# A fused retention and rational-MLP kernel: signs by a rectifier's slope, small constants in one transfer, 11 unread products, and a new early order

## The chip, the core and the metric

One core of a Trainium2 chip runs the whole program. The metric is device time in microseconds (us) of one execution, compared by the median of several. TensorE is called PE, VectorE DVE, ScalarE ACT, GpSimd POOL and SyncE SP, as in the profile. SP issues all data transfers. Each engine works through its own list of instructions in the order in which the program wrote them, and stops at an instruction whose inputs are not ready.

## What is computed

The reference first runs a retention layer: 8 batches, 8 heads, 576 tokens, 64 channels, with a decay per head in place of a softmax. Its output feeds a two-layer network with a rational function between the layers.

```
scores = (1/8) * q @ k^T;  ret = scores * Dmat[h]      # Dmat = gamma[h]^(i-j) for i >= j, else 0
x = (ret @ v) as [4608 tokens, 512]
h = x @ w_in                                           # w_in [512, 2048]
P = a0 + a1 h + a2 h^2 + a3 h^3
Q = 1 + |b0| |h| + |b1| h^2
out = (P / (Q + 1e-6)) @ w_out                         # w_out [2048, 512]
```

The two weight matrices arrive as 64-bit floats and are turned into 32-bit ones on the chip. All else is 32-bit.

## The kernel before

**Tiling.** The 4608 tokens are 36 units of 128 tokens (`NU`), and 9 blocks of 512 tokens (`NB`). A unit's q and k come as one transfer of 512 KB (`qk`), its k and v in the other layout as another (`kv`). Each of the 16 column groups of a weight matrix (`NF`) is a transfer of 512 KB (`bits`). An operand of the two large products is split in a high and a low part, so a step (one block, one column group) makes 12 products of 128x512 for `h` and 12 for the output `acc`. There are 144 steps.

**The early stage.** The first 8 units (`EARLY`) go through `attention`. For each: `scale_q` (POOL, q times a table `gq`), `scores` (PE), `decay` (DVE, mask), `scale_v` (DVE, v times a table `gv`), `outputs` (PE: `ps<-s,kv` and `ps<-kv`), `cross` (PE, with the state `S_sb`), `keep_hi` (ACT, `xhi`) and `keep_lo` (DVE, `xlo`), `grow` (DVE, adds to `S_sb`) and `fade` (POOL, scales `S_sb`). Cross of unit n waits for the fade of the unit before, so the units form a chain. Two PSUM buffers (`acc`) hold two units at a time. The first 4 units make block 0. Between these units stand the first steps.

**Weights.** `weight` turns one `bits` tile into a high and a low part. `begin` (ACT) takes the absolute value of the high words and scales it, `digit` (ACT) takes bits out of the low words into a tile `t`, `join` (DVE) shifts and ors the two, `sign` (DVE) ors the sign bit back, `high_part` (ACT, sometimes DVE) and `low_part` (POOL or DVE) make `w`.

**A step.** `feed_forward` writes the two products and between them, on ACT and DVE: `p_begin` (a3 h + a2), `size` (|h|), `p_mul`, `p_mul2`, `v_line` (b1 u + b0), `v_mul`, `log`, `exp`, `quot`, `check`, `better`, `g_hi`, `g_lo`. The first 24 steps are `early` (`IN_BANK`). `v_mul` of the first four is on POOL (`V_POOL`). The other 28 units are handled by `late_visit` between steps.

**What sets the order.** Nothing waits for an explicit schedule at run time. While the program is built, `Plan.run` plays the queues: every task has a due time (`DUE`, `FIRST`, `UNITS`), a cost and predecessors, and at each turn the engine that could start soonest writes its next instruction. `LOADS` sets the order of the early transfers. So `DUE`, `FIRST`, `LOADS`, the costs in `add` and the lags (`LAG`, `BACK`) together set the order on each engine.

**The start.** `WARM` products of zeros by zeros into a PSUM tile `unread` run before any data is there. Every instruction is recorded at line 71, the line of a helper, so tiles and not lines tell instructions apart.

Of the kernel before, what the change touches and what calls it, by code (L numbers as in the profile page):

```python
# [34 lines left out]
V_POOL = range(4)  # L35
IN_BANK = 24
WARM = 8
AHEAD = -6
REACH = 7.4
FIRST = (-30.37, -29.34, -25.59, -24.33, -24.08, -16.98, -16.13, -17.66)  # L40
UNITS = (20.48, 2.58, -2.5)
LATE = {'scale': -1.0, 'decay': 0.201, 'middle': 0.3, 'grow': 0.524, 'fade': 0.6, 'keep_hi': 0.3, 'keep_lo': 0.5}
LEAD = -2.2
CNV = 3
CNT = 1
SHIFT = 60
LOADS = 'w0 0 gq mask 1 w1 gv 2 w2 3 w4 w5 w3 5 4 ab w7 6 w9 w6 w10 w8 7 w11'.split()
# [53 lines left out]
class Plan:  # L101
# [19 lines left out]
    def run(self):  # L121
# [14 lines left out]
        dma, left, now, reach = 0.0, len(self.tasks), -2.0, REACH  # L136
        while left:
            best = None
            for e, queue in wait.items():
                found = []  # L140
                for t in queue:
                    if e != "SP" and t.due > now + reach:
                        continue
                    names = [r for r, _ in t.takes]
                    ready = [self.rings[r].ready(names[:j].count(r)) for j, r in enumerate(names)]
                    if None in ready:
                        continue
                    _, _, shared, hold = t.ways[e]
# [45 lines left out]
def retention_ffn(ctx: ExitStack, tc: tile.TileContext, qk, kv, w_in, w_out, ab, masks, masks2, gq, gv, out):  # L194
# [8 lines left out]
    cnt = ctx.enter_context(tc.tile_pool(name="cnt", bufs=CNT))  # L203
# [13 lines left out]
        "qk": 2, "kv": 2, "xp": 2, "cnv": CNV, "t": CNT, "v": 2, "u": 2, "p": 3, "g": 3, "o0": 1, "o1": 1,  # L217
# [12 lines left out]
    qc = const.tile([P, 1], F32, name="qc")  # L230
# [27 lines left out]
    bits, parts, joins = {}, {}, []  # L258
# [3 lines left out]
    def weight(order, s, w, f, loaded):  # L262
# [7 lines left out]
        def begin():  # L270
            c_[0] = cnv.tile([P, DM], I32, tag="c", name=f"c{nm}")
            act.activation(c_[0].bitcast(F32), words()[1].bitcast(F32), AF.Abs, scale=math.ldexp(1.0, -112))

        def digit():
            c_[1] = cnt.tile([P, DM], I32, tag="t", name=f"t{nm}")
            act.activation(c_[1], words()[2], AF.Copy, scale=15 * 2.0**-17)

        def join():
            dve.scalar_tensor_tensor(c_[0], c_[0], 3, c_[1], ALU.logical_shift_left, ALU.bitwise_or)

        def sign():
            dve.scalar_tensor_tensor(c_[0], words()[1], -0x80000000, c_[0], ALU.bitwise_and, ALU.bitwise_or)
# [16 lines left out]
        def low_part_v():  # L299
# [3 lines left out]
        t = add("ACT", d + DUE["begin"], 0.55, begin, [loaded], [("cnv", k)])  # L303
        t = add("ACT", d + DUE["digit"], 0.55, digit, [t], [("t", k)])
        t = add("DVE", d + DUE["join"], 0.61, join, [t], [], [("t", k)], True)
        joins.append(t)
        t = add("DVE", d + DUE["sign"], 0.61, sign, [t], shared=True)
        hi = add("ACT", d + DUE["high_part"], 0.53, high_part, [t], other=[("DVE", 0.5, high_part_v, True)])
        w_ready[k] = hi, add(
            "POOL", d + DUE["low_part"], 1.21, low_part, [hi], [], [("cnv", k)], True, [("DVE", 0.61, low_part_v, True)]  # L310
# [20 lines left out]
    def load_unit(n, due, after=()):  # L331
# [4 lines left out]
        def of(w, nm):  # L336
# [12 lines left out]
            add("SP", due + 0.01 * w, 524 / 390.0, of(w, nm), after, [] if late else [(nm, n)])  # L349
# [9 lines left out]
    def scale(n, at_, got, consts):  # L359
        def scale_q():  # L360
            q, _ = qk_of(n)
            pool.tensor_tensor(q, q, gq_sb, ALU.mult)

        def scale_v(by=dve):
            _, v = kv_of(n)
            dec = gv_sb[:, (n >= EARLY) * H : (n >= EARLY) * H + H].unsqueeze(2).broadcast_to([P, H, D])
            by.tensor_tensor(v, v, dec, ALU.mult)

        def scale_v_p():
            scale_v(pool)  # L370

        tq = add("POOL", at_(DUE["scale_q"]), 1.21, scale_q, [got[0], consts["gq"]], shared=True)
        tv = add("DVE", at_(DUE["scale_v"]), 0.6, scale_v, [got[1], consts["gv"]], shared=True,
                 other=[("POOL", 1.21, scale_v_p, True)])
        return tq, tv

    def attention(n, d, gap, got, consts, prev):
# [121 lines left out]
        th = add("ACT", at_(DUE["keep_hi"]), 0.5, keep_hi, done, [("xp", b)] if n % 4 == 0 else [], gives,  # L499
# [27 lines left out]
    def visit(n):  # L527
        m, heads = n + 1, [(j, g) for j in range(2) for g in range(NPAIR)]
        if "ps" not in late_s:
# [5 lines left out]
        if m < NU:  # L535
            bank["s"] = ps_h.tile([P, 512], F32, tag="h", name=f"ps{n}")
# [15 lines left out]
        if n >= EARLY:  # L552
# [17 lines left out]
    def decay(n):  # L570
        scr[n] = cnv.tile([P, 2, NPAIR, D], F32, tag="c", name=f"s{n}")
# [52 lines left out]
    def late_visit(n, d, got, consts, prev, hold):  # L624

        old, m = n >= EARLY, n + 1
        new, u = m < NU, (n + 1) % 9
        tq = tv = None
        if new:
            dn = d + LATE["scale"]  # L630
            tq = add("POOL", dn, 1.21, lambda: pool.tensor_tensor(qk_of(m)[0], qk_of(m)[0], gq_sb, ALU.mult),
# [7 lines left out]
            def scale_v_p():  # L639
# [3 lines left out]
                     other=[("POOL", 1.21, scale_v_p, True)])  # L643
        key = f"ps{n}"
        tm = te = None
        if m in sooner:
            tm = add("DVE", d - 1.5, 0.42, named(middle, m), [prev["visit"], prev.get("fade")])
        if n + 2 in sooner:
# [14 lines left out]
            "PE", d, (1.7 if m in sooner and n % 9 != 8 else 2.2) if old and new else 1.2, named(visit, n),  # L663
# [355 lines left out]
```

## Time and profile before

| | us |
|---|---|
| median of 3 runs | 899.9 (898.13 to 900.02) |
| the profiled execution | 900.45 |
| its span, first to last instruction | 898.6 |
| PE busy in it | 882.8 (98%) |
| DVE, ACT, POOL busy | 790.4, 653.2, 163.7 |

The page gives busy time per engine, then 40 slices of the span, the transfer queues, the chain of work that ended last, and the costliest groups of instructions. Rows of a timeline read: start, length, engine, line, operation, output<-input, count, and in brackets the idle time of the engine just before and what ended it. Two instructions that follow each other on ACT or DVE overlap a little, so the distance of their starts is some 0.1 us below the length of one.

### The profile page before, as it was taken

How to read it: one execution, taken by the hardware profiler on the slowest of the kernel's cores; microseconds unless marked ns; L12 is line 12 of the kernel's file. 1: busy time of each engine (PE TensorE's matmuls, PEld its weight loads, DVE VectorE, ACT ScalarE, POOL GpSimd, SP SyncE). 2: the span in 40 equal slices, each digit the busy share in tenths (PEclk: the TensorE clock that was granted, in tenths of full speed). 3: DMA queues.
4: the chain of work that ended last, by engine and by line, in shares of the span. 5: the costliest groups of instructions: out<-in, count | busy, mean ns of one | idle time of the engine just before them, and what ended most of it. 6: DMA issues, size and time to landing. Idle time of an engine off the chain costs nothing.

```text
span 898.6 us, 17725 instructions
## 1 busy us (share of the span) xinstructions
PE 882.8 (98%) x7344; PEld 730.3 (81%) x7344; DVE 790.4 (88%) x1215; ACT 653.2 (73%) x1019; POOL 163.7 (18%) x141
## 2 busy tenths in 40 slices
PE   6999999999999999999999999999999999999998
PEld 5777888887888888888888888888888888888886
DVE  4899999988999888988989888988888888987976
ACT  3589999965667767666766677767676786767765
POOL 3565664522211100011101110001100001000000
PEclk9999999999999999999999999999999999999999
DMA  9991000033311112111211131112211021001001
GB/s 357 407 406 69 1 1 1 0 112 123 109 49 61 58 34 70 41 47 60 95 48 48 59 107 48 48 47 74 80 48 47 26 74 44 1 1 47 1 1 47
DMA packets 22641, 67.41 MB, mean 75 GB/s; under 512 B 2592, under 2 KB 4512, under 8 KB 22560
## 3 DMA queue, kind: packets, MB, share of 16 engines
q1 hardware_dynamic: 22560, 66.28, 20.6%
q8 instruction: 57, 0.93, 0.4%
q14 instruction: 24, 0.20, 0.1%
HBM read 56.83 MB, written 9.44 MB: 74 GB/s over the span
## 4 chain that ended last, share of the span: by engine, by line
PE 92%; DVE 3%; DMA 3%; issue 0%; SPq 0%; ACT 0%; POOL 0%; ACTq 0%; DVEq 0%; POOLq 0%
PE acc L71 42%; PE h L71 42%; PE ps L71 7%; DMA bits<-in_w_in 2%; DVE p L71 1%; DMA kv<-in_kv 1%; SPq L71 0%; DVE c L71 0%; DVE s L71 0%; DVE kv L71 0%; DVE xlo L71 0%; DVE v L71 0%; ACT xhi L71 0%; ACT o L71 0%; DVE g L71 0%
## 5 line engine op out<-in xcount | busy, mean ns | idle before, releaser
L71 PE MATMUL acc<-w,g 128*128 128x512 f32 x1632 | 394.2, 390 | 0.0
L71 PEld LDWEIGHTS acc<-w,g 128*128 128x128 f32 x1632 | 305.5, 188 | 64.2 <-POOL w L71 0.4
L71 PE MATMUL h<-xhi,w 128*128 128x512 f32 x1152 | 310.6, 392 | 0.8 <-DVE p L71 0.7
L71 PEld LDWEIGHTS h<-xhi,w 128*128 128x128 f32 x1152 | 213.9, 188 | 47.4 <-DVE p L71 2.1
L71 ACT ACTIVATE p<-h,ab_sb 128x512 f32<-128x512 f32 x143 | 110.8, 775 | 90.7 <-PE h L71 88.5
L71 PE MATMUL h<-xlo,w 128*128 128x512 f32 x576 | 154.2, 390 | 0.0
L71 DVE TENSOR_TENSOR p<-p,h 128x512 f32<-128x512 f32 x144 | 98.4, 683 | 53.8 <-ACT u L71 50.9
L71 DVE SCALAR_TENSOR_TENSOR p<-p,ab_sb,h 128x512 f32<-128x512 f32 x168 | 124.5, 744 | 10.6 <-ACT u L71 8.0
L71 PEld LDWEIGHTS h<-xlo,w 128*128 128x128 f32 x576 | 108.1, 188 | 23.0
L71 ACT ACTIVATE g<-p 128x512 fp32r<-128x512 f32 x136 | 85.6, 629 | 46.5 <-DVE p L71 44.3
L71 ACT ACTIVATE u<-v,qc 128x512 f32<-128x512 f32 x120 | 86.7, 723 | 44.4 <-DVE v L71 44.4
L71 ACT ACTIVATE v<-u,absb 128x512 f32<-128x512 f32 x124 | 101.1, 815 | 3.6
L71 DVE SCALAR_TENSOR_TENSOR p<-p,ab_sb,u 128x512 f32<-128x512 f32 x120 | 95.7, 798 | 4.3 <-ACT u L71 4.3
L71 ACT ACTIVATE u<-h 128x512 f32<-128x512 f32 x144 | 84.8, 589 | 10.5 <-DVE v L71 5.7
L71 DVE SCALAR_TENSOR_TENSOR p<-v,p 128x512 f32<-128x512 f32 x120 | 86.4, 720 | 3.9
L71 DVE TENSOR_TENSOR v<-v,u 128x512 f32<-128x512 f32 x120 | 83.1, 693 | 4.3 <-ACT v L71 3.2
L71 DVE SCALAR_TENSOR_TENSOR v<-v,u 128x512 f32<-128x512 f32 x120 | 84.6, 705 | 0.0
L71 DVE TENSOR_TENSOR g<-p,g 128x512 fp32r<-128x512 f32 x112 | 77.3, 690 | 3.8 <-ACT g L71 2.9
L71 ACT ACTIVATE u<-u 128x512 f32<-128x512 f32 x120 | 75.0, 625 | 2.1
L71 POOL TENSOR_TENSOR qk<-qk,gq_sb 128x512 f32<-128x512 f32 x36 | 49.4, 1374 | 84.6 <-DMA qk<-in_qk 75.9
L71 PEld LDWEIGHTS ps<-qk 64*64 64x64 f32 (+1 forms) x1024 | 38.0, 146 | 18.8 <-issue 10.4
L71 POOL TENSOR_TENSOR S_sb<-S_sb,gv_sb 128x256 f32<-128x256 f32 x18 | 15.7, 872 | 191.7 <-DVE S_sb L71 190.0
(58 smaller groups left out, 766.3 us busy)
## 6 DMA issues: line engine op xcount, KB each, us to landing
qk<-in_qk SPq DMA_DIRECT2D x36, 512.0 KB, 3.9
kv<-in_kv SPq DMA_DIRECT2D x36, 512.0 KB, 5.2
bits<-in_w_in SPq DMA_DIRECT2D x16, 512.0 KB, 10.1
bits<-in_w_out SPq DMA_DIRECT2D x16, 512.0 KB, 10.2
out<-o SPq DMA_DIRECT2D x14, 512.0 KB, 3.3
out<-o SPq DMA_DIRECT2D x8, 256.0 KB, 2.3
x<-in_kv SPq DMA_DIRECT2D x7, 256.0 KB, 5.1
gq_sb<-in_gq SPq DMA_DIRECT2D x1, 256.0 KB, 6.5
```

The costliest lines, as they stand in the source:

```text
L71: return lambda *a, **k: self.tc.keep_in_program_order(method(*a, **k))
```

## The change

**Signs.** `begin` no longer takes an absolute value. It runs a parametric rectifier with slope -2^32 in place on the high words: a negative number comes out positive, with an exponent larger by 32, and the left shift by 3 in `join` puts that into the sign bit. `digit` writes in place too. `sign` and the tile `t` are gone: 32 DVE instructions.

**Small constants.** `gq`, `gv`, the second mask and `a`, `b` come as one array `factors` (602 columns, 301 KB) in one transfer, the first of all. There were four transfers.

**Operands of ACT.** In the early steps `p_begin` and in those not on POOL `v_line` multiply only, and the constant is added in `p_mul` and `v_mul`, which become three-operand instructions on DVE. `log` takes its constant as an immediate number, so the tile `qc` is gone.

**POOL.** `v_mul` of steps 0 to 5, 10, 11 and 17 is on POOL, where it was 0 to 3. All 32 low parts of weights are on POOL, where it was 28.

**Unread products.** `WARM` is 11, was 8.

**Order.** `LOADS`, `DUE`, `FIRST` and the lags have new values, and the queue model in `Plan.run` is changed: a limit of 8 outstanding transfers, two pauses of the transfer queue (`FETCH`), and a delay of DVE behind POOL (`PORT`). Of the tables two lines stand here, since their values tell a reader nothing. Code for visits of early units (`DENSE`, `VISITS`) is in the diff too, but with `DENSE = 8` and `VISITS = ()` it writes nothing.

```
-LOADS = 'w0 0 gq mask 1 w1 gv 2 w2 3 w4 w5 w3 5 4 ab w7 6 w9 w6 w10 w8 7 w11'.split()
+LOADS = 'gq 0 mask 1 0v 2 1v 2v 3 w0 5 3v 5v w2 w1 w5 4 w4 6 w3 w6 4v w9 w7 w11 w10 7v 7 6v w8'.split()
-V_POOL = range(4)
+V_POOL = (0, 1, 2, 3, 4, 5, 10, 11, 17)
-WARM = 8
+WARM = 11
...
-    mask2_sb = const.tile([P, D], F32, name="mask2_sb")
-    gv_sb = const.tile([P, 2 * H + NPAIR], F32, name="gv_sb")
-    gq_sb = const.tile([P, NPAIR, P], F32, name="gq_sb")
-    ab_sb = const.tile([P, 6], F32, name="ab_sb")
+    fac = const.tile([P, 512 + 2 * H + NPAIR + D + 6], F32, name="fac")
+    gq_sb = fac[:, 0:512].rearrange("p (g i) -> p g i", g=NPAIR)
...
         def begin():
+            x = words()[1].bitcast(F32)
+            act.activation(x, x, AF.Prelu, scale=math.ldexp(1.0, -112), alpha=-math.ldexp(1.0, 32))
+
+        def digit():
+            act.activation(words()[0], words()[2], AF.Copy, scale=15 * 2.0**-17)
+
+        def join():
             c_[0] = cnv.tile([P, DM], I32, tag="c", name=f"c{nm}")
-            act.activation(c_[0].bitcast(F32), words()[1].bitcast(F32), AF.Abs, scale=math.ldexp(1.0, -112))
-
-        def digit():
-            c_[1] = cnt.tile([P, DM], I32, tag="t", name=f"t{nm}")
-            act.activation(c_[1], words()[2], AF.Copy, scale=15 * 2.0**-17)
-
-        def join():
-            dve.scalar_tensor_tensor(c_[0], c_[0], 3, c_[1], ALU.logical_shift_left, ALU.bitwise_or)
-
-        def sign():
-            dve.scalar_tensor_tensor(c_[0], words()[1], -0x80000000, c_[0], ALU.bitwise_and, ALU.bitwise_or)
+            dve.scalar_tensor_tensor(c_[0], words()[1], 3, words()[0], ALU.logical_shift_left, ALU.bitwise_or)
...
-            act.activation(e["p"], hs[key], AF.Identity, bias=a2, scale=a3)
+            if early:
+                act.activation(e["p"], hs[key], AF.Copy, scale=a3)
...
-            dve.tensor_tensor(p, p, hs[key], ALU.mult)
+            if early:
+                dve.scalar_tensor_tensor(p, p, a2, hs[key], ALU.add, ALU.mult)
...
-            act.activation(e["line"], e["u"], AF.Identity, bias=b0, scale=b1)
+            if in_bank:
+                act.activation(e["line"], e["u"], AF.Copy, scale=b1)
...
-            (pool if v_pool else dve).tensor_tensor(e["v"], e["line"], e["u"], ALU.mult)
+            if in_bank:
+                dve.scalar_tensor_tensor(e["v"], e["line"], b0, e["u"], ALU.add, ALU.mult)
...
-            act.activation(e["r"], e["v"], AF.Ln, bias=qc)
+            act.activation(e["r"], e["v"], AF.Ln, bias=QC)
```

**Where instructions moved.** SP's first transfers, before. `qk_119` and `kv_121` are unit 0, `qk_125` and `kv_127` unit 1, `qk_134` unit 2, and `bits` are weights.

```order
L71 DMA bits_0_117<-in_w_in 128x512
L71 DMA qk_119<-in_qk 128x1024
L71 DMA kv_121<-in_kv 128x1024
L71 DMA gq_sb<-in_gq 128x512
L71 DMA mask_sb<-in_masks 128x320
L71 DMA qk_125<-in_qk 128x1024
L71 DMA kv_127<-in_kv 128x1024
L71 DMA bits_1_129<-in_w_in 128x512
L71 DMA gv_sb<-in_gv 128x20
L71 DMA qk_134<-in_qk 128x1024
```

The same place now. Unit 0 is `qk_116` and `kv_121`, unit 1 `qk_119` and `kv_125`, unit 2 `qk_123` and `kv_128`, unit 3's q and k `qk_130`, unit 5's `qk_135`.

```order
L77 DMA fac<-in_factors 128x602
L77 DMA qk_116<-in_qk 128x1024
L77 DMA mask_sb<-in_masks 128x320
L77 DMA qk_119<-in_qk 128x1024
L77 DMA kv_121<-in_kv 128x1024
L77 DMA qk_123<-in_qk 128x1024
L77 DMA kv_125<-in_kv 128x1024
L77 DMA kv_128<-in_kv 128x1024
L77 DMA qk_130<-in_qk 128x1024
L77 DMA bits_0_132<-in_w_in 128x512
L77 DMA qk_135<-in_qk 128x1024
```

The table `gq` moved from fourth to first (inside `fac`), and the first weight tile from first to tenth, behind the q and k of units 0 to 3.

DVE at units 2 and 3, before. Unit 2 is `ps_282`, unit 3 `ps_309` and `kv_145`; `c_2_266` is a weight tile.

```order
L71 TENSOR_TENSOR s_304<-ps_282,mask_sb 128x1024
L71 TENSOR_TENSOR s_339<-ps_309,mask_sb 128x1024
L71 TENSOR_TENSOR kv_145<-kv_145,gv_sb 128x512
L71 SCALAR_TENSOR_TENSOR c_2_266<-c_2_266,t_2_297 128x512
L71 TENSOR_TENSOR S_sb<-S_sb,ps_282 128x256
L71 TENSOR_TENSOR xlo_252<-ps_282,xhi_251 128x4x128
```

The same place now. Unit 2 is `ps_223`, unit 3 `ps_242` and `kv_146`, unit 5's k and v `kv_151`.

```order
L77 TENSOR_TENSOR s_240<-ps_223,mask_sb 128x1024
L77 SCALAR_TENSOR_TENSOR c_0_251<-bits_0_132 128x512
L77 TENSOR_TENSOR s_271<-ps_242,mask_sb 128x1024
L77 TENSOR_TENSOR S_sb<-S_sb,ps_223 128x256
L77 TENSOR_TENSOR kv_146<-kv_146,fac 128x512
L77 TENSOR_TENSOR kv_151<-kv_151,fac 128x512
L77 TENSOR_TENSOR xlo_188<-ps_223,xhi_187 128x4x128
```

The scaling of unit 3's v moved behind the state's growth by unit 2.

ACT at units 2 and 3 now: `xhi_187<-ps_223` is `keep_hi` of unit 2, `xhi_187<-ps_242` that of unit 3, and `bits_2`, `bits_1` are `begin` and `digit` of two weight tiles.

```order
L77 ACTIVATE w_0_274<-c_0_251 128x512
L77 ACTIVATE xhi_187<-ps_223 128x4x128
L77 ACTIVATE bits_2_179<-bits_2_179 128x512 x2
L77 ACTIVATE bits_1_184<-bits_1_184 128x512 x2
L77 ACTIVATE w_2_329<-c_2_318 128x512
L77 ACTIVATE xhi_187<-ps_242 128x4x128
```

Before, one conversion of a weight stood between these two; now five instructions on weights do, and two transfers must land for them.

## Rows read from the trace of the kernel before

**Rows 1.** The page: busy time of each engine, and the chain's shares.

```profile
PE 882.8 (98%) x7344; PEld 730.3 (81%) x7344; DVE 790.4 (88%) x1215; ACT 653.2 (73%) x1019; POOL 163.7 (18%) x141
PE 92%; DVE 3%; DMA 3%; issue 0%; SPq 0%; ACT 0%; POOL 0%; ACTq 0%; DVEq 0%; POOLq 0%
```

**Rows 2.** Windows: stretch, length, busy of five engines, granted clock, transfer share, GB/s.

```profile
0.00:10.00 10.00, 3.78 (x16) 3.49 (x16) 2.25 (x5) 3.12 (x4) 1.47 (x5) 1.00 0.83 293
10.00:20.00 10.00, 8.85 (x114) 8.24 (x114) 6.23 (x8) 2.40 (x4) 4.89 (x4) 1.00 1.03 410
57.00:100.00 43.00, 42.91 (x186) 34.54 (x187) 42.31 (x66) 42.71 (x74) 24.27 (x19) 1.00 0.34 135
100.00:140.00 40.00, 40.00 (x178) 33.14 (x177) 38.92 (x60) 39.15 (x67) 26.11 (x19) 1.00 0.00 1
```

**Rows 3.** Timeline of PE, from its first instruction to the fifth step.

```profile
1.06 3.78 PE L71 MATMUL unread<-S_sb 128*128 128x128 f32 x16 [1.06 <-DVE qc L71]
10.04 3.79 PE L71 MATMUL ps<-qk 64*128 64x128 f32 x32 [5.20 <-POOL qk L71]
14.05 1.97 PE L71 MATMUL ps<-s,kv 128*64 128x128 f32 x16 [0.22 <-DVE kv L71]
...
16.48 1.04 PE L71 MATMUL ps<-s,kv 128*64 128x128 f32 x16
...
18.88 1.09 PE L71 MATMUL ps<-qk,S_sb 64*64 64x128 f32 x16 [0.89 <-POOL S_sb L71]
22.52 1.16 PE L71 MATMUL ps<-qk 64*128 64x128 f32 x16 [1.45 <-POOL S_sb L71]
...
28.10 1.09 PE L71 MATMUL ps<-qk,S_sb 64*64 64x128 f32 x16 [0.42 <-POOL S_sb L71]
29.77 1.16 PE L71 MATMUL ps<-qk 64*128 64x128 f32 x16 [0.58 <-POOL qk L71]
...
37.27 1.09 PE L71 MATMUL ps<-s,kv 128*64 128x128 f32 x16 [0.59 <-DVE s L71]
...
56.95 1.20 PE L71 MATMUL h<-xhi,w 128*128 128x512 f32 x4 [0.17 <-DVE p L71]
```

**Rows 4.** Timeline of ACT and POOL: instructions that waited for a transfer.

```profile
4.38 0.66 ACT L71 ACTIVATE c<-bits 128x512 f32<-128x512 f32 x1 [2.36 <-DMA bits<-in_w_in]
8.73 1.26 POOL L71 TENSOR_TENSOR qk<-qk,gq_sb 128x512 f32<-128x512 f32 x1 [8.28 <-DMA gq_sb<-in_gq]
10.38 1.27 POOL L71 TENSOR_TENSOR qk<-qk,gq_sb 128x512 f32<-128x512 f32 x1 [0.39 <-DMA qk<-in_qk]
12.88 0.68 ACT L71 ACTIVATE c<-bits 128x512 f32<-128x512 f32 x1 [5.11 <-DMA bits<-in_w_in]
```

**Rows 5.** Timeline of DVE, ACT and POOL: steps of the units' chain.

```profile
12.17 1.23 DVE L71 TENSOR_TENSOR s<-ps,mask_sb 128x1024 f32<-128x1024 f32 x1 [3.68 <-PE ps L71]
17.33 0.42 DVE L71 COPY S_sb<-ps 128x256 f32<-128x256 f32 x1 [1.60 <-ACT xhi L71]
17.68 0.68 DVE L71 TENSOR_TENSOR kv<-kv,gv_sb 128x512 f32<-128x512 f32 x1
26.93 0.42 DVE L71 TENSOR_TENSOR S_sb<-S_sb,ps 128x256 f32<-128x256 f32 x1 [0.79 <-ACT xhi L71]
16.70 0.60 ACT L71 ACTIVATE xhi<-ps 128x512 fp32r<-128x512 f32 x1 [2.59 <-PE ps L71]
21.74 0.61 POOL L71 TENSOR_TENSOR S_sb<-S_sb,gv_sb 128x256 f32<-128x256 f32 x1 [1.69 <-DMA bits<-in_w_in]
```

**Rows 6.** Groups by line and shape, whole span: count, busy, mean ns of one, idle before.

```profile
L71 DVE SCALAR_TENSOR_TENSOR c<-bits,c 128x512 int32<-128x512 int32 x32 | 23.0, 718 | 0.2
L71 ACT ACTIVATE u<-h 128x512 f32<-128x512 f32 x144 | 84.8, 589 | 10.5 <-DVE v L71 5.7 <-DVE p L71 3.9
L71 ACT ACTIVATE p<-h,ab_sb 128x512 f32<-128x512 f32 x143 | 110.8, 775 | 90.7 <-PE h L71 88.5 <-DVE g L71 1.5
L71 POOL TENSOR_TENSOR v<-v,u 128x512 f32<-128x512 f32 x4 | 5.9, 1485 | 0.8 <-ACT v L71 0.8
```

More of the change, by code (lines that the diff above doesn't have):

```diff
@@ L57 @@
-HOLD = {('POOL', 'scale_v'): 3.0, ('DVE', 'p_begin'): 0.616, ('DVE', 'high_part'): 0.5, ('DVE', 'g_hi'): 1.221, ('DVE', 'keep_hi'): 1.153, ('DVE', 'g_lo'): 99.0, ('DVE', 'low_part'): 1.002, ('POOL', 'v_mul'): 0.229}
+LAG = {'PE': 0.21, 'ACT': 0.138, 'DVE': 0.118, 'POOL': 0.08, 'SP': 0}
+BACK = {'PE': 0.21, 'ACT': 0.0, 'DVE': 0.0, 'POOL': 0.0, 'SP': 0.0}
+ENTER = {'PE': 0.03, 'ACT': 0.0, 'DVE': 0.0, 'POOL': 0.045, 'SP': 0.0}
+PORT = 0.33
+FETCH = ((4.8, 1.0), (15.5, 1.1))
+DUE = {'p_begin': -0.998, 'size': 1.908, 'p_mul': -0.347, 'p_mul2': 5.296, 'v_line': 1.475, 'v_mul': 1.541, 'log': 3.284, 'exp': -0.985, 'quot': 1.963, 'check': 2.017, 'better': -1.338, 'g_hi': 1.445, 'g_lo': -1.676, 'gemm2': 4.596, 'begin': -0.512, 'digit': 1.055, 'join': -0.091, 'high_part': 1.387, 'low_part': 6.778, 'scale_q': 0.308, 'scale_v': 1.347, 'scores': 2.952, 'decay': 0.786, 'outputs': 6.305, 'cross': -5.06, 'keep_hi': -5.352, 'keep_lo': 3.008, 'grow': -0.794, 'fade': 1.051}
@@ L135, in run @@
         port = {"DVE": 0.0, "POOL": 0.0}
[L136 removed]
+        dma, landed, left, now, reach = 0.0, [0.75] * OUTSTANDING, len(self.tasks), -2.0, REACH
         while left:
@@ L175, in run @@
             if e == "SP":
-                clock["SP"] = s + 0.43
-                dma = max(dma, s + 1.4) + cost
-                t.end = dma + 1.0
+                clock["SP"] = s + 0.47
+                fetch = sum(x for at, x in FETCH if dma < at <= max(dma, s + 1.5) + cost)
+                dma = max(dma, s + 1.5) + cost + fetch
+                t.end = dma + 0.8
+                landed.append(t.end)
             else:
@@ L302, in weight @@
         d = min(s - LEAD, AHEAD + order)
[L303 to L308, printed above, removed]
+        t = add("ACT", d + DUE["begin"], 0.56, begin, [loaded])
+        t = add("ACT", d + DUE["digit"], 0.56, digit, [t])
+        t = add("DVE", d + DUE["join"], 0.6, join, [t], [("cnv", k)], shared=True)
+        hi = add("ACT", d + DUE["high_part"], 0.52, high_part, [t], other=[("DVE", 0.5, high_part_v, True)])
         w_ready[k] = hi, add(
-            "POOL", d + DUE["low_part"], 1.21, low_part, [hi], [], [("cnv", k)], True, [("DVE", 0.61, low_part_v, True)]
+            "POOL", d + DUE["low_part"], 1.25, low_part, [hi], [], [("cnv", k)], True, [("DVE", 0.6, low_part_v, True)]
         )
@@ L622, in named, with late_visit @@
         return emit
-    def late_visit(n, d, got, consts, prev, hold):
-        old, m = n >= EARLY, n + 1
-        new, u = m < NU, (n + 1) % 9
+    def late_visit(n, d, got, consts, prev, hold, old=True, new=True):
+        m, u = n + 1, (n + 1) % 9
+        early = m <= EARLY and not (new and m == EARLY)
         tq = tv = None
@@ L646, in late_visit @@
         if m in sooner:
-            tm = add("DVE", d - 1.5, 0.42, named(middle, m), [prev["visit"], prev.get("fade")])
+            tm = add("DVE", d - 1.5, 0.33, named(middle, m), [prev["visit"], prev.get("fade")])
         if n + 2 in sooner:
```

196 lines of the change are left out of this document (110 added, 86 removed).

## The prediction

> **What bounds the kernel now.** I read the page first. PE is busy for 882.8 of 898.6 us, and the chain that ended last runs 92% through PE [rows 1]. So the time is PE's work plus the time in which PE has nothing to do or works at a lower rate. Next come the windows, to see where that is. In the first 10 us PE is busy for 3.78, all of it unread products, and in the next ten for 8.85; from 57 to 100 it is 42.91 of 43 and from 100 to 140 all of 40 [rows 2]. PE's timeline puts names to it [rows 3]: the first scores start at 10.04, after 5.20 us of waiting for POOL's scaling of q; then come waits of 0.22, 0.89, 1.45, 0.42, 0.58, 0.59 and 0.17 until the fifth step starts at 56.95. After that there is next to nothing to win but the tail, which the change leaves alone.
>
> A second loss hides in busy time. The 16 products of unit 0's first output take 1.97 us at 14.05, those of unit 1 take 1.04 at 16.48, and the first 32 score products take 3.79 where 16 take 1.16 later [rows 3]. The granted clock reads 1.00 (the level of 2.4 GHz) in every window [rows 2], so that column doesn't show it, but the durations say that PE ran at about half its rate (the level of 1.2 GHz) from its first instruction, through a pause of 5.2 us, and for some six further microseconds of nearly unbroken work.
>
> The transfers explain the wait. The first weight tile lands just before 4.38, but `gq`, fourth in the queue, only before 8.73, and POOL waits for that one [rows 4]. From 10 us on the queue moves 410 GB/s [rows 2], which is 1.28 us for 512 KB; the two transfers between 10.38 and 12.88 bear that out (1.25 each) [rows 4].
>
> **The start.** The new first transfer has 301 KB in place of 512, so it lands 0.53 us earlier than the weight tile did, near 3.85, and q of unit 0 1.28 later, at 5.13. POOL needs 1.26 and PE starts 0.05 after it [rows 3, 4]: scores 0 at 6.45 instead of 10.04. The other bound: counting back from 8.73 over 256 and 512 KB puts the old second transfer at 6.8, but counting forward from 4.38 puts it at 5.66 [rows 4]. Some 1.15 us were lost in the queue between these two; if that falls on q now, scores 0 start at 7.6. I take 6.45, since the forward count starts from a row. The 11 unread products hide in the wait: 3.78 us for 8 [rows 3] make 5.2 for 11, from 1.06 to 6.25. Without that cover they would cost up to 1.4.
>
> Later landings I count from 8.73, so that the lost time is inside: q1 7.96, kv0 9.24, q2 10.5, kv1 11.8.
>
> Now unit 0 and 1, once at the high rate from scores 0 on, once at the low one. Scores 0 end at 7.6 (low 8.4); decay takes 1.23 and starts 0.22 after [rows 3, 5]: done 9.05 (9.8). Then v is scaled, 0.68 [rows 5], not before kv0 is there: 9.9 (10.5). Scores 1 wait for POOL until 9.25 and end at 10.4 (11.15). Outputs 0 start at 10.5 (11.2); it was 14.05. They take 1.5 us, as those of unit 1 did, or 2.4 at the low rate (14.05 to 16.48): 12.0 (13.6). From there to cross 1 stand `keep_hi`, the copy of the state and its fade. The copy started 0.85 after outputs 0 (17.33, the products ending near 16.5); 0.42 for it, 0.1 to change engines and 0.61 to 1.0 for the fade [rows 5] give cross 1 at 14.1. Outputs 1 fit before it: kv1 at 11.8, scaled by 12.5, done by 14.0. At the low rate decay 1 ends at 12.6, outputs 1 at 15.1 to 16.0, and cross 1 comes at 15.6 to 16.1. Before it was 18.88. **Gain up to here: 4.8, or 3.0 at the low rate.**
>
> **From cross 1 to the fifth step.** Before, the waits in this stretch add to 1.45 + 0.42 + 0.58 + 0.59 + 0.17 = 3.2 [rows 3]. In the new order I find three. Scores 3 need the PSUM buffer of unit 1: cross 1 (1.09), `keep_hi` 0.60, growth 0.42 and `xlo` 0.68 end some 0.75 after scores 2; it was 1.45, since a join and a sign (0.72 for the sign alone [rows 6]) no longer stand in front. Outputs 3 get a new wait: the scaling of unit 3's v now stands behind the growth by unit 2, which before started 0.79 us after DVE was free, once ACT had kept unit 2 [rows 5]. So after cross 2 come 0.75 + 0.42 + 0.68, some 1.8 us, before outputs 3 can start, and the wait of 0.42 at cross 3 goes, as the fade runs beside them. Queued behind that growth on DVE are both scalings of v, `xlo` of unit 2 and a join; PE waits for the first. The wait of 0.58 for q at scores 5 goes: its load is seven places earlier and POOL has scaled it long before. I put 0.3 for the rest. Sum 2.9, a gain of 0.3.
>
> **What is moved and costs nothing there.** The signs: 32 instructions of 718 ns [rows 6], 23.0 us of DVE. With five `v_mul` and four low parts moved to POOL (0.7 each) and 39 instructions that become three-operand ones (0.06 each), DVE loses some 27 us. ACT: two operands read from a tile cost 775 - 589 = 186 ns [rows 6], so 93 each; some 60 of them go, 6 us. POOL gains nine instructions of 1.3 to 1.5 us [rows 6], some 13. In 57 to 140 us DVE and ACT are over 97% busy and PE loses 0.09 [rows 2]. So this is room, not gain: PE arrives there 4 us earlier and needs it, since the same work must be done sooner. The rectifier itself isn't in the trace; its bounds are ACT's shortest and longest pass over 128x512, 0.59 and 0.78 [rows 6], and I take 0.66, the length of the instruction it replaces [rows 4]. Its 32 passes at the upper bound would cost 3.5 us of ACT, less than the 6 it gains. Fewer, larger transfers take three issues off SP, which is ahead of the data anyway.
>
> **The sum.** 4.8 + 0.3 = 5.1 at the high rate, 3.0 + 0.3 = 3.3 at the low one. PE no longer pauses 5.2 us before scores 0, but pauses short of 1 us twice, so I expect the rise somewhere inside units 0 and 1 and take the middle, 4.2. The profiled execution took 900.45, so 896.2; it stands 0.55 above the median of 899.9, so the median should be 895.7.
>
> **Rivals.** *The high rate from scores 0.* Unread products now fill PE nearly until scores 0. If the rise comes in them, the gain is 5.1, and 6.4 if the wait at outputs 3 is half as long: 893.5 to 894.8. Against it: 3.78 us of the same products left the rate low before [rows 3]. For it: they end 0.2 us before scores 0, not 5.2. The Trainium skill, page "TensorE: Matmul & The Clock Gate", section "The HAM clock gate (the 'warmup' mystery)", says that a clock gate lets half the pulses through until PE has been busy for a while, and that the point of the rise differs between runs of one kernel; by that rule this rival would be the forecast. The same section says that clock events in traces have been unreliable, with which the column of 1.00 beside durations twice as long agrees.
>
> *Behind the loads.* ACT keeps unit 3 only after `begin` and `digit` of two weight tiles, which land by my count near 21.7 and 23.0, and outputs 4 wait for kv4, moved back to near 31.9. My chain needs them at 24 to 25 and at 33. Two more losses of about 1.1 us, like the one above, put both on PE's path: the gain falls to about 1.2, the time to 898.7.
>
> *Slower: POOL's share of a step.* `v_mul` takes 1.49 us on POOL [rows 6] against 0.7 on DVE, and there it stands behind low parts of 1.3 us. If two of these come in front, a step's chain is 2 x 1.3 + 0.8 = 3.4 us longer. PSUM has four buffers for `h` in this stretch, so PE waits when the delay eats what they hold. It decides from the second of the added steps 4, 5, 10, 11, 17: with three of them on PE's path the loss is 10, against 4.2 gained, and the time 905.7. Against it: steps 0 to 3 did this before without a wait of PE after 57 us, and POOL is busy 24.27 of 43 and 26.11 of 40 us there [rows 2].
>
> *It doesn't bring the start forward:* if q0 lands late and its unread products run past it, unit 0 is no earlier than kv0 allows and the low rate stays through unit 2; what remains is some 1 us, 899.
>
> **Chances.** Forecast (gain 2.5 to 5) 0.52; high rate from scores 0 0.20; behind the loads 0.16, half of it under a gain of 1.8; POOL 0.07; start not earlier 0.05. A measurement of this kernel can tell about 0.2%, 1.8 us, from no change. So faster 0.52 + 0.20 + 0.08 = 0.80, the same 0.08 + 0.05 = 0.13, slower 0.07. The range reaches from the high rate with half the wait at outputs 3, 893.5, to the loads rival, 898.7; outside are POOL and parts of the last one, and of the first.
>
> **What would show it.** PE's timeline should have scores 0 between 6.4 and 7.6, outputs 0 near 10.5 to 11.2, cross 1 at 14 to 16, a wait of DVE at the growth by unit 2 and one of PE, 1.5 to 2 us, before outputs 3, and the fifth step's first product near 52.8. The rise of the rate is where 16 score products take 1.16 and not 1.9. No PE wait should stand between 57 and 140; a wait there for DVE's `p` or POOL's `g` would mean the POOL rival. A wait for ACT's `xhi` at the first `h` near 26 would mean the loads. ACT's passes over `bits` should stay below 0.78.

## The result, and the profile after

The changed kernel takes 906.42 us (median of four runs, 905.54 to 907.24) against 899.64 for the kernel before beside it: a ratio of 1.0078 with an interval of 1.0061 to 1.0096. It is slower by 0.8%, where I had forecast 895.7 and put 0.07 on slower.

The page of the profile after (span 905.2 us, executed in 907.24): busy time of PE, DVE, ACT and POOL, and the chain's shares. They answer to [rows 1].

```profile
PE 887.2 (98%) x7350; PEld 732.3 (81%) x7350; DVE 777.4 (86%) x1175; ACT 636.4 (70%) x1017; POOL 173.0 (19%) x150
PE 80%; DVE 9%; ACT 8%; issue 1%; DMA 1%; POOL 1%; SPq 0%; ACTq 0%; DVEq 0%; POOLq 0%
```

DVE and ACT have less to do, 13.0 and 16.8 us, and yet they stand on the chain for 9% and 8%, where it was 3% and nothing. The windows say where (columns as in [rows 2]):

```profile
57.00:100.00 43.00, 41.37 (x182) 33.61 (x180) 37.68 (x53) 38.23 (x67) 27.05 (x22) 1.00 0.34 135
100.00:140.00 40.00, 38.63 (x168) 31.38 (x169) 34.45 (x51) 38.22 (x68) 25.92 (x21) 1.00 0.00 1
180.00:190.00 10.00, 8.85 (x158) 7.03 (x159) 7.04 (x12) 4.63 (x9) 2.85 (x2) 0.66 0.01 2
```

From 57 to 140 PE was idle for 0.09 us before; now it is for 3.0. DVE has 4.6 and 4.5 us less to do in these two windows, ACT 4.5 and 0.9: they are less busy and later. In the last window the granted clock reads 0.66.

PE's timeline names the waits. The first part answers to [rows 3], the part from 71.63 on has no row there, because there was no wait.

```profile
6.79 1.16 PE L77 MATMUL ps<-qk 64*128 64x128 f32 x16 [0.66 <-POOL qk L77]
9.65 1.72 PE L77 MATMUL ps<-qk 64*128 64x128 f32 x16 [1.70 <-POOL qk L77]
...
15.75 1.09 PE L77 MATMUL ps<-qk,S_sb 64*64 64x128 f32 x16 [0.51 <-POOL S_sb L77]
18.86 1.16 PE L77 MATMUL ps<-qk 64*128 64x128 f32 x16 [0.93 <-POOL S_sb L77]
24.36 1.09 PE L77 MATMUL ps<-s,kv 128*64 128x128 f32 x16 [1.82 <-DVE kv L77]
...
52.61 1.19 PE L77 MATMUL h<-xhi,w 128*128 128x512 f32 x4
...
71.63 1.19 PE L77 MATMUL h<-xhi,w 128*128 128x512 f32 x4 [0.84 <-DVE p L77]
99.91 1.19 PE L77 MATMUL h<-xhi,w 128*128 128x512 f32 x4 [0.79 <-DVE p L77]
104.11 0.73 PE L77 MATMUL acc<-w,g 128*128 128x512 f32 x2 [1.19 <-ACT o L77]
105.02 2.56 PE L77 MATMUL acc<-w,g 128*128 128x512 f32 x10 [0.18 <-ACT o L77]
181.15 1.12 PE L77 MATMUL ps<-kv 64*64 64x64 f32 x16 [2.67 <-DVE p L77]
182.20 5.49 PE L77 MATMUL acc<-w,g 128*128 128x512 f32 x12
```

The start came out nearly as worked out. What was lost lies behind it: 0.84 + 0.79 + 1.19 + 0.18 + 2.67 = 5.67 us of waiting, and products at half their rate after the last wait (5.49 us for twelve, which take 3.02 in a run below). The waits cost a little more than their length: around each of the four between 71 and 105 PE's products start some 0.27 us later than the idle time alone makes them, 1.1 in all. The product at 181.15 is the first of the late visits; it goes into a PSUM bank that the last early step, step 23, holds until DVE has made its `better`.

DVE's and POOL's timelines show what is long now. First the joins of weights (`c<-bits`) and one product of `v` on DVE, then what POOL does at the same time:

```profile
72.41 2.95 DVE L77 SCALAR_TENSOR_TENSOR c<-bits 128x512 int32<-128x512 int32 x3
86.65 4.09 DVE L77 SCALAR_TENSOR_TENSOR c<-bits 128x512 int32<-128x512 int32 x3
143.50 2.39 DVE L77 SCALAR_TENSOR_TENSOR c<-bits 128x512 int32<-128x512 int32 x2
176.52 1.78 DVE L77 TENSOR_TENSOR v<-v,u 128x512 f32<-128x512 f32 x1
```

```profile
86.95 1.54 POOL L77 TENSOR_TENSOR g<-p,g 128x512 fp32r<-128x512 f32 x1 [6.17 <-ACT g L77]
88.60 3.31 POOL L77 TENSOR_TENSOR w<-c,w 128x512 fp32r<-128x512 f32 x2
176.47 1.28 POOL L77 TENSOR_TENSOR w<-c,w 128x512 fp32r<-128x512 f32 x1 [0.92 <-ACT w L77]
```

A join alone takes 0.68 (at 139.27 in the same profile). The three at 86.65 are not slowed alike: the first takes 0.68, it begins 0.30 before POOL's `g`; the other two begin 0.30 and 0.36 behind an instruction of POOL's and take 1.78 each:

```profile
87.25 1.78 DVE L77 SCALAR_TENSOR_TENSOR c<-bits 128x512 int32<-128x512 int32 x1
88.96 1.78 DVE L77 SCALAR_TENSOR_TENSOR c<-bits 128x512 int32<-128x512 int32 x1
```

POOL's three take 1.54 to 1.66 in place of 1.3. Of the three at 72.41 one is slowed (1.75), of the two at 143.50 one (1.79), and the product at 176.52 begins 0.05 after POOL's and takes 1.78. These five instructions make the four places some 5.4 us longer.

Before, a join (`c<-c,t`) and the `sign` behind it (`c<-bits,c`) stood mostly singly in this stretch, with two to four others of DVE's between them; now joins come in rows of three and two. Here is one pair of before:

```profile
83.49 0.68 DVE L71 SCALAR_TENSOR_TENSOR c<-c,t 128x512 int32<-128x512 int32 x1
85.47 0.68 DVE L71 SCALAR_TENSOR_TENSOR c<-bits,c 128x512 int32<-128x512 int32 x1
```

The kernel before was not free of it: three of its joins took 1.73 to 1.77, all ahead of 50 us. From 57 us on its longest join or `sign` took 1.13.

### The profile page after: what moved, and what is told of

Read it like the earlier page. It is cut to its first block, busy times and chain, and to the rows that moved or that the text cites. A ratio compares the mean times of both kernels' runs of the same rounds, so it can differ in the third digit from the quotient of the medians.

```text
span 905.2 us, 17712 instructions
## 1 busy us (share of the span) xinstructions
PE 887.2 (98%) x7350; PEld 732.3 (81%) x7350; DVE 777.4 (86%) x1175; ACT 636.4 (70%) x1017; POOL 173.0 (19%) x150
## 4 chain that ended last, share of the span: by engine, by line
PE 80%; DVE 9%; ACT 8%; issue 1%; DMA 1%; POOL 1%; SPq 0%; ACTq 0%; DVEq 0%; POOLq 0%
PE h L77 36%; PE acc L77 36%; PE ps L77 8%; DVE p L77 4%; ACT h L77 2%; ACT bits L77 2%; DVE c L77 1%; ACT u L77 1%; DVE v L77 1%; ACT p L77 1%; DVE h L77 1%; DMA qk<-in_qk 1%; ACT w L77 1%; ACT g L77 1%; ACT xhi L77 0%
## 5 line engine op out<-in xcount | busy, mean ns | idle before, releaser
L77 ACT ACTIVATE p<-h,fac 128x512 f32<-128x512 f32 x141 | 107.6, 763 | 103.7 <-PE h L77 102.7
L77 DVE SCALAR_TENSOR_TENSOR p<-p,fac,h 128x512 f32<-128x512 f32 x192 | 142.2, 744 | 20.4 <-ACT u L77 12.3
L77 DVE TENSOR_TENSOR p<-p,h 128x512 f32<-128x512 f32 x120 | 82.2, 685 | 43.2 <-ACT u L77 40.7
L77 ACT ACTIVATE v<-u,absb 128x512 f32<-128x512 f32 x129 | 105.3, 816 | 3.9
L77 ACT ACTIVATE u<-v 128x512 f32<-128x512 f32 x120 | 75.7, 631 | 40.5 <-DVE v L77 40.5
L77 DVE SCALAR_TENSOR_TENSOR p<-p,fac,u 128x512 f32<-128x512 f32 x120 | 92.8, 773 | 9.2 <-ACT u L77 5.4
L77 DVE SCALAR_TENSOR_TENSOR v<-v,u 128x512 f32<-128x512 f32 x120 | 90.2, 752 | 0.0
L77 DVE SCALAR_TENSOR_TENSOR p<-v,p 128x512 f32<-128x512 f32 x120 | 84.3, 703 | 3.4
L77 POOL TENSOR_TENSOR qk<-qk,fac 128x512 f32<-128x512 f32 x36 | 49.3, 1369 | 96.8 <-DMA qk<-in_qk 96.5
L77 POOL TENSOR_TENSOR S_sb<-S_sb,fac 128x256 f32<-128x256 f32 x18 | 14.7, 814 | 186.7 <-DVE S_sb L77 186.7
```

Of the source, the lines that this page charges most:

```text
L77: return lambda *a, **k: self.tc.keep_in_program_order(method(*a, **k))
```

## The experiments

All have the kernel before beside them (898.97 to 899.49 us over the three groups of runs); medians are given, and ratios with intervals where the verdict rests on them.

**The wait at 181.** Two runs take it first, since it looked like a matter of place.

```
-UNITS = (20.48, 2.58, -2.5)
+UNITS = (21.48, 2.58, -2.5)
```

> The changed kernel with the first visit of the late units due one step later (first value of UNITS 21.48 in place of 20.48), nothing else. Theory 'one wait and the clock': PE's wait of 2.67 us at 181 us and the 6.8 us at the low clock behind it are one event, set by a visit that stands too near the last early step. Then the wait shrinks below 1 us, no stretch of low clock follows, and the time falls by 5 to 6 us, to 901. Rival 'the order of the weights': the wait comes from DVE and ACT being late all along, so it moves with the visit and the time stays within 1 us of 906.4.

904.57 us, 1.0059 [1.0043, 1.0076]. The larger due time moved no instruction of PE: with the time planned for it the visit keeps its place in PE's order. What it moved are scalings of loads on POOL, and from 104 us on joins, lower parts and steps' instructions on DVE, ACT and POOL. The wait stayed:

```profile
181.93 0.68 PE L77 MATMUL ps<-kv 64*64 64x64 f32 x16 [2.96 <-DVE p L77]
```

Its sixteen products take 0.68 here, not 1.12: behind a wait that is even longer, no low rate followed in this execution. As a test of the place it says nothing.

The second run fills the wait, in the visit of the unit before the late ones, ahead of the product that waits:

```
...
+        fill = 11 if n == EARLY - 1 else 0
         for x in range(4 * NPAIR):
+            if x == 2 * NPAIR:
+                for _ in range(fill):
+                    pe.matmul(bank["s"][0:32], none, parts[0, 0][:, 0, :], start=False, stop=True, skip_group_check=True)
```

> The changed kernel with 11 products of zero weights (32x512, they add zero to scores already done) put into PE's list right before the instruction that waits 2.67 us at 181 us. They fill the wait and take nothing from it. If the low clock behind the wait costs by itself, the granted clock stays at 1.00 there, and the time falls by 3 to 3.4 us, to 903. If the low clock is a mere companion, the time stays at 906 to 907.

903.04 us, 3.4 less than the changed kernel, and the twelve products after the visit are back at full rate:

```profile
178.45 2.73 PE L77 MATMUL ps<-w,none 128*32 128x512 f32 x11
181.22 0.68 PE L77 MATMUL ps<-kv 64*64 64x64 f32 x16
181.83 3.02 PE L77 MATMUL acc<-w,g 128*128 128x512 f32 x12
```

The wait itself cost the same, filled or not. So the low rate was a cost of its own on top of the 2.67. From the first of the sixteen products to the end of the twelve it is 2.9 us in the two profiles (6.46 from 181.15 on, 3.56 from 181.22 on); the medians differ by 3.4, or by 2.7 if each is taken against the kernel before beside it.

**Order or operations.** The third run keeps the new operations and gives the planner before's due times, lags and loads (and its 8 unread products):

```
-V_POOL = (0, 1, 2, 3, 4, 5, 10, 11, 17)
+V_POOL = range(4)
...
-LAG = {'PE': 0.21, 'ACT': 0.138, 'DVE': 0.118, 'POOL': 0.08, 'SP': 0}
+LAG = {'PE': 0.25, 'ACT': 0.097, 'DVE': 0.217, 'POOL': 0.16, 'SP': 0}
...
-PORT = 0.33
+PORT = 0.0
...
```

> All arithmetic of the change (signs, constants in one transfer, operands of ACT), but the tables, lags and the order of loads of the kernel before, v_mul of four steps on POOL, 8 unread products. 'The order' theory: the edits cost nothing and give DVE room, the losses after 57 us come from the new order alone: 898 to 900, no wait of PE over 0.5 us between 70 and 190. Rival 'the edits': passes in place on ACT and three-operand instructions make the chain of a step longer, so waits appear here too: 903 or more.

913.16 us. That isn't before's order, only before's numbers: with other operations and costs the planner makes a third order of them, with a wait of its own at 106.94.

```profile
106.94 4.91 PE L77 MATMUL acc<-w,g 128*128 128x512 f32 x12 [5.55 <-ACT o L77]
```

So it does not part the two theories. What does is the run with four copies below, which keeps every new operation and has the time of the kernel before. The fourth takes back one line:

```
-V_POOL = (0, 1, 2, 3, 4, 5, 10, 11, 17)
+V_POOL = range(4)
```

> The changed kernel with v_mul of steps 4, 5, 10, 11, 17 back on DVE. My POOL rival: these five put 3.4 us each on a step's chain, so without them the waits at 71, 99 and 104 us (3.0 together) go and the time falls to 902 to 903.5. 'The order' theory: they are a small part, the weights' conversions in bursts remain: 905 to 908.

899.35 us, 1.0001 [0.9989, 1.0012]: 7 us less than the changed kernel. The waits at 71, 99 and 104 are gone, the one for DVE's `p` at the visit is 1.74. This seemed to bear out the POOL rival, and more strongly than I had expected. But the line does two things: it moves five products from POOL to DVE, and the planner makes a new order with them. The next two runs keep the order and move the products alone; PE's and ACT's instructions are the same one for one.

```
-                (pool if v_pool else dve).tensor_tensor(e["v"], e["line"], e["u"], ALU.mult)
+                (pool if i < 4 else dve).tensor_tensor(e["v"], e["line"], e["u"], ALU.mult)
```

> Every instruction of the changed kernel in its order on every engine (TensorE's and ScalarE's rows are the same one for one), but the product of line and u of steps 4, 5, 10, 11 and 17 is carried out by VectorE at the same place of the plan instead of GpSimd. If GpSimd's 1.3 us for each of them, with its queue ahead of it, is what makes better and g late (the first theory), the waits of 0.84 at 71.6, 0.79 at 99.9 and 1.19 at 104.1 us go or fall under 0.3, and the time is 900 to 903 us (the wait of 2.67 at 181 and its low clock may stay: step 17 is far from it). If it is the order that the new plan gives (the second theory), VectorE has five more instructions of about 0.7 us in the same order, the waits stay or grow by up to 0.7 each, and the time is 906 to 909 us.

```
-                (pool if v_pool else dve).tensor_tensor(e["v"], e["line"], e["u"], ALU.mult)
+                (pool if v_pool and i not in (4, 5) else dve).tensor_tensor(e["v"], e["line"], e["u"], ALU.mult)
```

> As the run before, but only steps 4 and 5 have that product on VectorE; 10, 11 and 17 stay on GpSimd, all else in the order of the changed kernel. First theory: the wait at 71.6 us (0.84) goes and those at 99.9 and 104.1 (0.79, 1.19) stay, or fall by what the start of their chain gained: 904.5 to 906 us. Second theory: the wait at 71.6 stays at 0.5 or more, 906 to 907.5 us. A third: all that is late comes from the first delay and is handed on from step to step; then the waits at 100 and 104 go with the one at 71, and the time is that of the run before.

904.83 and 905.99 us. The first time lies in neither of the ranges that I gave (900 to 903, 906 to 909), so the waits have to decide: they stayed, and the first grew. In the profile of the first run the visit's wait is 2.60, and the sixteen products behind it take 0.85 and not 1.12: less of the stretch behind it ran at the low rate. PE's and DVE's timelines of the run with all five on DVE:

```profile
72.95 1.20 PE L77 MATMUL h<-xhi,w 128*128 128x512 f32 x4 [1.75 <-DVE p L77]
101.28 1.19 PE L77 MATMUL h<-xhi,w 128*128 128x512 f32 x4 [0.82 <-DVE p L77]
105.48 0.73 PE L77 MATMUL acc<-w,g 128*128 128x512 f32 x2 [1.19 <-ACT o L77]
```

```profile
65.83 1.78 DVE L77 TENSOR_TENSOR v<-v,u 128x512 f32<-128x512 f32 x1
88.04 4.08 DVE L77 SCALAR_TENSOR_TENSOR c<-bits 128x512 int32<-128x512 int32 x3
```

So GpSimd's time for the five products isn't what costs at 100 and 104; my rival had its sign and its size by luck. For the wait near 72 these runs decide nothing: step 4's product takes 1.78 on DVE, more than the 1.29 that it took on POOL. The rows of joins are still there. This led to the theory of the next group: what costs is which DVE instructions lie beside POOL's.

**A better version on the way.** Two runs start from before's `V_POOL`. One fills the wait at the visit with products of zeros as the second run did, one has the later due time of the first run.

```
-V_POOL = (0, 1, 2, 3, 4, 5, 10, 11, 17)
+V_POOL = range(4)
...
+        fill = 7 if n == EARLY - 1 else 0
...
```

> The changed kernel with before's choice of steps for GpSimd (0 to 3, the plan made anew with it, as in the run that gave 899.35), and seven products of 128x32 zeros, 512 columns each, added to a sum ahead of the visit's first product that waited 1.74 us for VectorE's p at 176.3 us. If the low granted clock behind that wait (3.41 us of records at half) follows from the wait, it goes with the wait filled: 899.35 less half of 3.4 = 897.5 to 898 us, and the wait itself is under 0.3. If the low clock comes from something else it stays and the time is 899.3 to 900.

```
-V_POOL = (0, 1, 2, 3, 4, 5, 10, 11, 17)
+V_POOL = range(4)
...
-UNITS = (20.48, 2.58, -2.5)
+UNITS = (21.48, 2.58, -2.5)
```

> The changed kernel with before's choice of steps for GpSimd (0 to 3), and the first visit of the units due one step later (21.48 for 20.48), so that the product that waited 1.74 us at 176.3 stands about one step (5.4 us of TensorE's work) further from the last early step. If that wait is only a matter of that place, it goes and with it the low clock of 3.41 us behind it: 899.35 - 1.74 - 1.7 = 895.9 us, between 895 and 897. If the last early step's better is late for another reason and takes the visit with it, the wait is over 1 us again and the time 898.5 to 900.

The fill: 898.93 us (897.3 to 900.46), not to be told from 899.35 (897.3 to 901.49), though the wait and the low rate are gone in its profile. Inconclusive: the two programs scatter by 3 to 4 us. The later due time: 896.62 us, 0.9972 [0.9961, 0.9983], faster than the kernel before. Again it moved no instruction of PE, so my reason for it was wrong; from some 99 us on it moves scalings of loads on POOL behind weights' lower parts, and instructions on DVE and ACT, and with them what lies beside what. Which of these moves helps was not tried. In its profile the start runs at the high rate too (outputs 3 at 22.84, 24.57 in the profile of 899.35). The wait at the visit shrinks:

```profile
173.49 0.68 PE L77 MATMUL ps<-kv 64*64 64x64 f32 x16 [0.71 <-DVE p L77]
```

**Joins and POOL apart.** These two are the changed kernel with its order on every engine. Ahead of some of POOL's instructions stands a copy of one element of the last join's result, so that POOL starts when DVE's joins are done.

```
+            joined[0] = c_[0]
...
+    def behind():
+        pool.tensor_copy(glance, joined[0][0:1, 0:1])
...
         def g_lo(by=None):
             p, g = els.pop(key)["p"], gs[key]
+            if i in (4, 6, 17):
+                behind()
...
         def low_part(by=pool):
+            if 24.6 < d < 24.8:
+                behind()
```

> The changed kernel, every instruction in its order, with four copies of one element added on GpSimd: each reads the result of the last join that VectorE has been given, ahead of the g of steps 4, 6 and 17 and of one weight's lower part, so that GpSimd begins there only when VectorE's joins are done. In the changed kernel those joins lay beside GpSimd's work: 2.95 us for three at 72.4, 4.09 for three at 86.7, 2.39 for two at 143.5 and 1.78 for one product at 176.5, against 0.68 for one that lies alone. Theory (VectorE falls behind TensorE where its instructions lie beside GpSimd's): they take 2.05, 2.05, 1.36 and about 0.7 (5.1 us less); the waits at 99.9 (0.79), 104 (1.19 and 0.18) and 181 (2.67) go or fall under 0.5 each, with them the low clock (3.4); the wait at 71.6 (0.84), ahead of the first of them, stays; 906.4 - 0.8 - 1.4 - 2.7 - 3.4 = 898.1 us, between 897.5 and 901. Rival (TensorE's order asks too early, whatever VectorE's speed): the waits stay at 0.5 or more each, and the time is 904.5 to 907.

898.89 us, 0.9997 [0.9988, 1.0007]; 7.5 us less than the changed kernel, by four instructions more. DVE's, POOL's and PE's timelines:

```profile
71.24 1.89 DVE L77 SCALAR_TENSOR_TENSOR c<-bits 128x512 int32<-128x512 int32 x3
84.78 1.89 DVE L77 SCALAR_TENSOR_TENSOR c<-bits 128x512 int32<-128x512 int32 x3
88.91 2.17 DVE L77 SCALAR_TENSOR_TENSOR p<-p,fac,h 128x512 f32<-128x512 f32 x3 [0.25 <-ACT p L77]
139.73 1.29 DVE L77 SCALAR_TENSOR_TENSOR c<-bits 128x512 int32<-128x512 int32 x2
171.63 0.69 DVE L77 TENSOR_TENSOR v<-v,u 128x512 f32<-128x512 f32 x1
```

```profile
86.73 0.17 POOL L77 COPY glance<-c 1x1 int32<-1x1 int32 x1 [7.10 <-DVE c L77]
86.87 1.29 POOL L77 TENSOR_TENSOR g<-p,g 128x512 fp32r<-128x512 f32 x1
88.13 2.55 POOL L77 TENSOR_TENSOR w<-c,w 128x512 fp32r<-128x512 f32 x2
```

```profile
70.45 1.20 PE L77 MATMUL h<-xhi,w 128*128 128x512 f32 x4 [0.81 <-DVE p L77]
175.17 0.68 PE L77 MATMUL ps<-kv 64*64 64x64 f32 x16 [0.44 <-ACT u L77]
```

The four places take 5.76 us instead of 11.21. The waits at 99.9 and 104 are gone; of the 2.67 at the visit 0.44 is left and waits for ACT, and there is no low rate behind it. This profile stands 1.2 us earlier than that of the changed kernel from 52 us on, since its scores ran at the high rate; that is not the copies' doing. Beyond that POOL, held back, is none the later: its three instructions end at 90.68 where they ended at 91.91. The wait at 70.45, ahead of all of this, stayed, as expected.

```
...
+            if i in (6,):
+                behind()
```

> As the run before with only one of the four copies, ahead of the g of step 6: the three joins at 86.7 us take 2.05 for 4.09, the others stay as in the changed kernel. Theory: the waits at 99.9 and 104 us (0.79, 1.19, 0.18) go or fall under 0.4 each, and all after it comes as much earlier on both engines, so that the wait at 181 stays at 2.3 to 3 with its low clock: 906.4 - 2 = 904.4 us. Rival of the run before: 906 to 907, the waits unchanged. If all lateness were handed on from this one place, the wait at 181 would go too: 898 to 899.

902.42 us (one copy, ahead of step 6's `g`). The joins there take 1.89, the wait at 99.9 is gone, and what is left is as the theory has it:

```profile
100.81 0.73 PE L77 MATMUL acc<-w,g 128*128 128x512 f32 x2 [0.37 <-ACT o L77]
101.72 2.55 PE L77 MATMUL acc<-w,g 128*128 128x512 f32 x10 [0.18 <-ACT o L77]
177.83 0.68 PE L77 MATMUL ps<-kv 64*64 64x64 f32 x16 [2.67 <-DVE p L77]
```

So the three joins at 86 cost most of the waits at 100 and 104, and the wait at the visit belongs to the other three places, which were not tried singly. The gain was 4.0 where I expected 2.0. In its profile the sixteen products behind the wait of 2.67 take 0.68 and not 1.12, and the granted clock is 0.83 on average over 174 to 184: a shorter stretch at the low rate, which gives back 1.3. There too the start ran at the high rate, which gives 1.4.

**The last two** are on the version of 896.62: the same copy ahead of the lower part at the visit, and 8 unread products in the place of 11.

```
...
         def low_part(by=pool):
+            if 24.6 < d < 24.8:
+                behind()
```

> The version that gave 896.62 (five products back on VectorE, the visits one step later) with one copy of one element on GpSimd ahead of the weight's lower part that lay beside VectorE's product of 1.79 us at 168.9. By the theory that product takes 0.7, the wait of 0.71 for VectorE's p at 173.5 goes, and the time is 896.6 - 0.7 = 895.9 us; if the wait has another cause it stays, at 896.6.

```
...
-WARM = 11
+WARM = 8
...
```

> The version that gave 896.62 with 8 unread products at the start in the place of 11. If the three more are what makes the first scores run at the high rate in some executions (1.2 to 1.35 us for 2.1), all executions fall to the low rate: up to 1.6 us more, 898.0 to 898.5, and the lowest of the runs is near 897.5. If the rate at the start comes out either way whatever they are, the time is 896.3 to 897.2.

The copy: 896.36 us, 0.9971 [0.996, 0.9981]; the product of 1.79 us and the wait of 0.71 are gone from the profile, with the same order on PE, ACT and DVE; the 0.26 us lie within what the runs scatter. It beats both kernels, as its parent does. With 8 unread products the time is 898.41, 1.8 more. PE's timelines, with 8 (an execution of 900.5 us, the slowest of its ten) and with 11 (the run with the copy):

```profile
8.20 3.96 PE L77 MATMUL ps<-qk 64*128 64x128 f32 x32 [3.68 <-POOL qk L77]
13.18 1.97 PE L77 MATMUL ps<-s,kv 128*64 128x128 f32 x16 [1.02 <-DVE kv L77]
```

```profile
6.89 1.16 PE L77 MATMUL ps<-qk 64*128 64x128 f32 x16 [1.62 <-POOL qk L77]
9.70 1.16 PE L77 MATMUL ps<-qk 64*128 64x128 f32 x16 [1.65 <-POOL qk L77]
10.79 1.09 PE L77 MATMUL ps<-s,kv 128*64 128x128 f32 x16
```

Here q of unit 0 also came 1.3 us later with 8, so not all of the 1.8 is the rate's; but 16 score products take 1.98 with 8 and 1.16 with 11, and in the runs of this study with 11 they took 1.16 to 2.08, different from execution to execution of nearly the same start.

## Why the prediction was wrong

- **The start was right.** Scores 0 at 6.79 (forecast 6.45), cross 1 at 15.75 (15.6 to 16.1 at the low rate), a new wait before outputs 3 of 1.82 (1.8), scores 3 with 0.93 (0.75), the fifth step's first product at 52.61 (52.8). The rate fell back after scores 0 (1.16, then 1.72 and 1.97), so the gain came out near the 3.3 of the low case, some 0.9 less than the middle that I took. Cross 1 is 3.1 earlier than before; of the 4.3 at the fifth step's first product 1.0 is no gain, since a cross product that stood ahead of it before now stands behind it (54.95).
- **The high rate from scores 0** is no fiction: in the profiles of four runs with the same 11 products sixteen score products take 1.16 to 1.35, and outputs 3 start at 22.55 to 22.98 in place of 24.36. In the profile of the changed kernel it wasn't so.
- **The rectifier** takes 670 ns, in the bounds (0.66). ACT lost 16.8 us where I had 6: I left out the 120 later `log`s, which lost their tile operand too (723 to 631 ns, 11.0 us). POOL gained 9.3 where I had 13. DVE lost 13.0 of busy time where I had 27; but my 27 added up lengths, and instructions overlap a little. By lengths it lost 20.4. The signs' 23.0 are gone; I missed that the 120 later products of `v` went from 705 to 752 ns (5.6 us).
- **"Room, not gain" is the step that failed.** I took 27 us less work on DVE and 6 less on ACT as room, put the cost of the new order behind the start at nothing, and wrote that no PE wait should stand between 57 and 140; 3.0 us of such waits do. I counted busy time per engine and compared sums. Whether an engine is in time depends on what it does between a step's `h` and its `better`, and on what POOL does meanwhile; the sum says neither. The new plan puts joins in rows of two and three where POOL works. The planner knows of this: its tasks marked `shared` may not lie beside one another on DVE and POOL (`port`). But that holds in its own time only; on the chip the joins and POOL's work did meet, and both were slowed. How far the planner's times were off isn't shown. That the four places cost it is shown by the run with four copies: with everything else in place, waits of 0.79, 1.37 and 2.23 of 2.67 go and with the last the low rate of 2.9, 7.3 us together; the medians differ by 7.5.
- **The POOL rival** named the sign (905.7) and the wrong mechanism: the products' own length. With the products moved back to DVE in the same order the time is 904.83. Before's choice of steps helps (899.35) because another order follows from it, in which 32 joins take 752 ns on average and not 860. A share of the rival may stand in the wait of 0.81 to 0.84 near 71, which no hold took away and before's `V_POOL` did; it was not tried by itself.
- **No term held the rate after a wait.** I let waits cost their length. The one at 181 cost 2.67 and some 3 more. It lies behind 140, where I had not looked for a loss at all.

The sum of after against the forecast for the profiled execution, 907.24 - 896.2 = 11.0: waits 5.67 and the 1.1 around them, low rate 2.9, start 0.9; 0.4 is not placed.

## What to carry to other kernels

Less busy time on two engines is no promise while a third waits for one chain of them: look at what lies beside what, and where DVE with both operands in SBUF may meet POOL, count its instruction at the slow length (here 1.8 us for 0.7). When a table that sets an order is made anew, compare the neighbours in the order on DVE and POOL before the sums. A collision can be parted without a new plan, by one tiny instruction on the engine that is to wait.

## What the runs showed of the hardware

- **DVE beside POOL.** With both operands in SBUF (a join, or `v` by `u`), 128x512 takes DVE 0.68 to 0.69 alone, and 1.75 to 1.79 at the five places of the changed kernel where it began 0.05 to 0.36 behind a POOL instruction. The join at 86.65, which began 0.30 ahead of POOL's, took 0.68. With one operand in PSUM it isn't slowed: three `p<-p,fac,h` take 2.17 at 88.91 in the run with four copies, beside POOL's 2.55 at 88.13. The Trainium skill, page "SBUF — State Buffer", section "SBUF: two separate sides", says that DVE with two SBUF inputs and POOL lock a shared pair of ports against each other for a whole instruction. The rows agree: the product of 1.78 is 0.69 and 1.09 of POOL's 1.28, which began 0.05 earlier.
- **TensorE's rate after a wait.** After 2.67 us of waiting in the changed kernel the granted clock stood at 0.66 on average over 180 to 190 (the level of 1.2 GHz for part of it), and twelve products took 5.49. In other runs it fell too after 1.74 (0.88 over 170 to 180), 2.60 (0.83 over 180 to 190) and 2.67 (0.83 over 174 to 184), and after 2.96 and 2.97 in two others it read 1.00. In these runs, all but that of 1.74 with the same order on PE, the length of the wait alone doesn't settle it; what does stays open. Filled with products, the wait left the rate as it was.
